# A transformer block on one core: small work moved behind the row maxima, GpSimd in a written order, and the last phase's weights loaded and split one step apart

## The chip, the core and the metric

The kernel runs on one core of a Trainium2 chip. A core has five engines with their own instruction queues: TensorE (PE in the profile, its weight loads PEld), VectorE (DVE), ScalarE (ACT), GpSimd (POOL) and SyncE (SP), which only issues DMA transfers. Each queue runs in order, and an instruction that has to wait holds everything behind it on its engine. Engines meet through semaphores. The metric is the device time of one execution in microseconds, a median of several runs.

## The reference

The output is `x + attention(xn) + glu(xn)`, with `xn` the layer norm of `x` (2048 rows of 640, float32):

```python
xn = _layernorm(x)                                   # rows of 640
q, k, v = split(xn @ wqkv)                           # 32 heads of 20
scores = einsum("bhqd,bhkd->bhqk", q, k) * 20 ** -0.5
scores = where((i - j >= 0) & (i - j < 256), scores, -1e9)
attention = einsum("bhqk,bhkd->bhqd", softmax(scores), v) @ wo
glu = (gelu(xn @ w_gate) * (xn @ w_up)) @ w_down     # 1728 wide
out = x + attention + glu
```

## The kernel before

Every float32 product is made of three matmuls: both operands are split in a high part (a ScalarE copy to `F32R`) and a low part (the remainder, a subtraction on VectorE or GpSimd), and high·high, low·high and high·low are added up in PSUM.

The kernel has four stretches in time. The first (to about 88 us) makes the layer norm and the first projections. The second, `attention()` (about 88 to 660 us), works through 32 units `u`: eight groups of four heads times four chunks of 512 rows. Each unit has `NS = 14` slots, and `now[0]` counts slots. TensorE's order in a slot is written out: on even slots two score pieces for the exponentials (`exp_piece`, PSUM tag `ex`, two buffers) and two or three pieces for the row maxima of a unit further on (`max_piece`, tag `mx`, three buffers); in every slot about three steps of a filler (`pull_fill`): the projections of q, k and v and the gate and up products of the GLU. At slot 0 of the next unit comes `av_unit`, probabilities times `v`.

Small work hangs on a table `acts`, from slot to functions: `defer(n, fn)` puts `fn` n slots later, and `tick()` hands out what is due at the start of a slot, ahead of the slot's score and maximum pieces. There:

- `max_piece` (L428) computes scores into PSUM; VectorE's `tensor_tensor_reduce` (L444) adds the mask and takes the row maximum. A PSUM buffer is free again when VectorE has read it.
- `max_end` (L453) turns the negated maxima with one matmul (L456), ScalarE copies them to `mr` (L458), and SyncE sends them into two rows of the unit's `qs` (L459), where the score matmuls add them.
- `save_qk` (L215) drains a projection: ScalarE's copy `upper` (L236), VectorE's remainder (L237), ScalarE's second copy (L224), GpSimd's last remainder (L225), then stores to `qd` or `kd` (L231).
- `gate_up_fill` (L550) makes GELU by hand in steps `c1` to `c5`, alternating ScalarE and VectorE, and stores to `hd` (L581).
- `load_stack` (L414) reads `qd` and `kd` back for unit `u + 3` (six DMAs, L422).
- `exp_piece` (L483) takes the exponential on ScalarE (L496) and clears with GpSimd's `affine_select` (L502, L505) what lies outside the window, in three banks of probabilities.
- `av_unit` (L509) copies its result on ScalarE (L520) and stores it by five DMAs (L522, L523).
- `load_v` (L245) loads and splits the second half of the v weights; `x_sums` (L619) makes sums of `xn` on GpSimd (L643) and stores them (L646).

`tc.manual_schedule(engines=MANUAL)` keeps TensorE, ScalarE and VectorE in the written order there; GpSimd's and SyncE's instructions are placed by the framework's scheduler.

The third stretch (660 to 843 us) makes the rest of gate and up in pairs of chunks. The fourth, the last phase (from 843 us), is the product with `w_down` and `wo`: 80 steps `n`, ten for each of eight blocks `p` of 256 rows, one of the ten an `"e"` step with eight matmuls. A "plain" step (all of `p = 0`, the first four of `p = 1`) has 24 matmuls of 320 columns; every other has 21, with sums of operands in seven products, Strassen's way. Step `n` loads the operand of step `n + 4` (L1029, buffers `hr`), splits that of `n + 2` (`split_step`, three buffers `at`), splits a weight quad of 128 x 1280 if one is due (`high_quad` on ScalarE, L930, in step `n`; `low_quad` on VectorE, by `sub`, L937, in step `n + 1`) and fetches another quad (`fetch`, L915, three buffers `stg`). The quads `b4` to `b8` are first used in steps 5 to 9, the quads `t4` to `t8` from step 15 on, `t0` to `t3` from step 26 on. After a block's last step `drain` adds the PSUM banks to the output rows on VectorE, and TensorE must wait for a bank to be added up before the next block writes to it.

Of the kernel before, what the change touches and what calls it, by code (L numbers as in the profile page):

```python
# [24 lines left out]
NF = 14  # L25
# [36 lines left out]
def block_kernel(ctx, tc, x, wqk, wv, wgu, wdo, wdl, out):  # L62
# [131 lines left out]

    def defer(n, fn, *a):
        if now[0] is None:
            fn(*a)
        else:
            at(now[0] + n, fn, *a)
# [17 lines left out]
    def save_qk(t, c, ps):  # L217
# [5 lines left out]
        def lower():  # L223
            nc.scalar.activation(pt[:, 1, :], r, AF.Copy)  # L224
            nc.gpsimd.tensor_tensor(out=pt[:, l, :], in0=r, in1=pt[:, 1, :], op=OP.subtract)  # L225
            a, end = t % 5 * 128, t % 5 * 128 + 128
# [7 lines left out]

        def upper():
            nc.scalar.activation(pt[:, h, :], ps, AF.Copy)  # L236
            nc.vector.tensor_tensor(out=r, in0=ps, in1=pt[:, h, :], op=OP.subtract)  # L237
            defer(1, lower)
# [3 lines left out]
    def load_v(h, res, rpool=None):  # L242
# [185 lines left out]
    def max_piece(u, i):  # L428
# [5 lines left out]
        ps = psm.tile([128, 384], F32, name="ps_m", tag="mx")  # L434
# [11 lines left out]
        if i == 15:  # L446
            mx = maxes.pop(u)
            nm = nms[u % 2]
            nc.vector.tensor_scalar(nm[:, 0, 0], mx, -1.0, None, op0=OP.mult)
            nc.vector.scalar_tensor_tensor(nm[:, 0, 1], mx, -1.0, nm[:, 0, 0], op0=OP.mult, op1=OP.subtract)  # L450
            maxes[u] = nm

    def max_end(u):  # L453
# [5 lines left out]
        nc.sync.dma_start(qs[u % NQ][120:122].rearrange("p j t -> p (j t)"), mr)  # L459
# [20 lines left out]
    def exp_piece(u, s):  # L480
# [16 lines left out]
        if j == 3:  # L497
            for p in bank:
                for col, diag in diag_tail(*p, c):
                    a = pt[:, :, col:col + 128]  # L500
                    if diag:
                        nc.gpsimd.affine_select(out=a, in_=a, pattern=[[0, 4], [1, 128]], compare_op=OP.is_ge,  # L502
                                                fill=0.0, base=0, channel_multiplier=-1)
                    else:
                        nc.gpsimd.affine_select(out=a, in_=a, pattern=[[0, 4], [-1, 128]], compare_op=OP.is_ge,  # L505
                                                fill=0.0, base=-1, channel_multiplier=1)

    def av_unit(u):
# [12 lines left out]
        for j in range(4):  # L521
            nc.sync.dma_start(od[c].rearrange("(d h) t -> h d t", h=H)[4 * g + j], ob[32 * j:32 * j + DH, :])  # L522
        nc.sync.dma_start(sd[c][4 * g:4 * g + 4, :], ob[DH::32, :])  # L523
# [27 lines left out]
    def gate_up_fill(f, ws, c):  # L551
# [4 lines left out]
        def c1():  # L556
# [4 lines left out]
            defer(1, c2)  # L561
# [809 lines left out]
```

## Time and profile before

| | |
|---|---|
| three runs | 1089.28, 1089.98 and 1090.28 us; median 1089.98 us |
| the profiled execution | 1090.18 us, its span 1088.4 us |
| granted TensorE clock | 0.999 |
| TensorE busy | 1070.2 us, 98% of the span, 7253 matmuls |
| VectorE, ScalarE, GpSimd busy | 762.3, 511.8 and 334.6 us |
| all DMA | 162.31 MB, 149 GB/s on average |

Matmuls are pipelined, and the profile models their ends, so two neighbours overlap on paper and a busy TensorE is not one at its peak. "Idle before" an instruction is the time in which its engine had nothing in work, with what ended it. SyncE's rows are its sequencer's: an issue, and not the transfer.

### The profile page before, as it was taken

Reading aid. Unit: us, or ns where it says so; the run is one execution under the profiler, and the core shown is the slowest. Engines: PE = TensorE matmul, PEld = TensorE weight load, DVE = VectorE, ACT = ScalarE, POOL = GpSimd, SP = SyncE. Lnnn points to the kernel's source line nnn. Section 1 sums busy time; section 2 is a strip of 40 time slices with the busy share of each in tenths; the row PEclk is TensorE's granted clock in tenths of the full one; section 3 lists DMA queues with packets and bytes.
Section 4 is the critical chain, followed back from the end, with each engine's and each line's share of the span. In section 5 each row is a group of like instructions: output and inputs, shape, how many; then the busy total and the mean of one; then the engine's idle time right before and its main releaser. Section 6 shows DMA issues by size and latency. Waiting matters only on the chain.

```text
span 1088.4 us, 20870 instructions
## 1 busy us (share of the span) xinstructions
PE 1070.2 (98%) x7253; PEld 856.8 (79%) x7253; DVE 762.3 (70%) x2030; ACT 511.8 (47%) x1037; POOL 334.6 (31%) x513
## 2 busy tenths in 40 slices
PE   8999999999999999999999999999999999999998
PEld 7887667666678766666666677888888999999998
DVE  7756667566666575666666636788775779888887
ACT  4434655465645456555555465332223554333332
POOL 5045634566726444655344241121110000000000
PEclk9999999999999999999999999999999999999999
DMA  5642343446442333353332316488775884343443
GB/s 202 200 137 82 114 142 92 129 130 181 142 132 65 94 109 117 117 163 104 111 112 84 98 51 203 150 279 292 242 256 177 281 289 163 92 137 121 134 125 115
DMA packets 96058, 162.31 MB, mean 149 GB/s; under 512 B 13248, under 2 KB 57920, under 8 KB 95952
## 3 DMA queue, kind: packets, MB, share of 16 engines
q1 hardware_dynamic: 95952, 160.97, 46.8%
q8 instruction: 57, 0.93, 0.4%
q14 instruction: 49, 0.40, 0.1%
HBM read 104.40 MB, written 56.23 MB: 148 GB/s over the span
## 4 chain that ended last, share of the span: by engine, by line
PE 80%; DVE 9%; DMA 4%; ACT 3%; issue 2%; SPq 1%; POOL 1%; DVEq 0%; ACTq 0%
PE ps_d L101 23%; PE ps L1100 16%; PE ps_g L844 14%; PE ps_o L516 7%; PE ps_e L494 7%; PE ps_m L442 7%; PE ps_v L101 5%; PE ps_g L101 1%; DVE junk L444 1%; DVE ss L937 1%; DMA hr<-od 1%; ACT P L496 1%; DMA od<-ato 1%; DVE at L937 1%; ACT at L1054 1%
## 5 line engine op out<-in xcount | busy, mean ns | idle before, releaser
L444 DVE CUSTOM_DVE_ANT_0 junk<-ps_m,mask 128x384 bf16<-128x384 f32 (+2 forms) x512 | 271.8, 531 | 177.4 <-PE ps_m L442 136.2
L496 ACT ACTIVATE P<-ps_e 128x512 f32<-128x512 f32 (+2 forms) x384 | 197.6, 568 | 63.6 <-PE ps_e L494 57.4
L1100 PE MATMUL ps<-wb,at 128*128 128x320 f32 x999 | 156.9, 310 | 3.3 <-DVE xr L1120 2.8
L1100 PEld LDWEIGHTS ps<-wb,at 128*128 128x128 f32 x999 | 148.9, 188 | 4.5 <-DVE xr L1120 3.3
L502 POOL TENSOR_SCALAR_AFFINE_SELECT P<-P 128x512 f32<-128x512 f32 x128 | 83.7, 654 | 176.4 <-ACT P L496 169.2
L101 PE MATMUL ps_d<-xh,wql 128*128 128x512 f32 x430 | 129.3, 410 | 0.0
L101 PE MATMUL ps_d<-xl,wqh 128*128 128x512 f32 x430 | 128.6, 408 | 0.0
L101 PE MATMUL ps_d<-xh,wqh 128*128 128x512 f32 x430 | 128.5, 409 | 0.0
L442 PE MATMUL ps_m<-ks,qs 120*128 120x128 bf16 (+1 forms) x704 | 120.9, 275 | 3.6 <-DVE mx L444 1.8
L494 PE MATMUL ps_e<-qs,ks 122*128 122x128 bf16 (+2 forms) x704 | 113.1, 277 | 1.5 <-ACT P L496 0.8
L494 PEld LDWEIGHTS <-ks 122*128 122x128 bf16 x704 | 50.2, 98 | 55.2 <-issue 44.5
L101 PEld LDWEIGHTS ps_d<-xh,wql 128*128 128x128 f32 x430 | 77.9, 189 | 15.8 <-issue 2.3
L101 PEld LDWEIGHTS ps_d<-xl,wqh 128*128 128x128 f32 x430 | 78.3, 188 | 14.8 <-issue 0.6
L1100 PE MATMUL ps<-wt,at 128*128 128x320 f32 x552 | 89.1, 309 | 0.0
L101 PEld LDWEIGHTS ps_d<-xh,wqh 128*128 128x128 f32 x430 | 77.7, 189 | 14.1 <-ACT xh L185 0.3
L442 PEld LDWEIGHTS <-qs 120*128 120x128 bf16 x704 | 62.1, 98 | 32.7 <-issue 13.8
L516 PE MATMUL ps_o<-P,v 128*32 128x384 f32 (+2 forms) x1408 | 84.3, 386 | 0.0
L505 POOL TENSOR_SCALAR_AFFINE_SELECT P<-P 128x512 f32<-128x512 f32 x112 | 72.3, 656 | 37.3 <-ACT P L496 37.3
L1100 PEld LDWEIGHTS ps<-wt,at 128*128 128x128 f32 x552 | 82.9, 188 | 0.3 <-DVE u L937 0.3
L1054 ACT ACTIVATE at<-ss 128x512 fp32r<-128x512 f32 x59 | 37.3, 632 | 90.1 <-DVE ss L937 89.8
L516 PEld LDWEIGHTS ps_o<-P,v 128*32 128x32 f32 x1408 | 40.1, 110 | 39.5 <-issue 29.2
L225 POOL TENSOR_TENSOR pt<-r,pt 128x512 bf16<-128x512 f32 x40 | 46.7, 1168 | 79.2 <-ACT pt L224 79.1
(185 smaller groups left out, 1692.8 us busy)
## 6 DMA issues: line engine op xcount, KB each, us to landing
hr<-hd SPq DMA_DIRECT2D x104, 128.0 KB
hd<-he SPq DMA_DIRECT2D x50, 256.0 KB
wr<-wgu SPq DMA_DIRECT2D x27, 320.0 KB
qs<-qd SPq DMA_DIRECT2D x32, 240.0 KB
ks<-kd SPq DMA_DIRECT2D x32, 240.0 KB
ats<-wdo SPq DMA_DIRECT2D x9, 640.0 KB
wtd<-ats SPq DMA_DIRECT2D x9, 640.0 KB
stg<-wtd SPq DMA_DIRECT2D x9, 640.0 KB
```

The source lines that it names most:

```text
L101: nc.tensor.matmul(ps, a(k), b(k), start=n == 0, stop=n == 3 * nk - 1)
L225: nc.gpsimd.tensor_tensor(out=pt[:, l, :], in0=r, in1=pt[:, 1, :], op=OP.subtract)
L442: nc.tensor.matmul(ps[:, lo:hi], lh, rhs, start=True, stop=True)
L444: nc.vector.tensor_tensor_reduce(out=junk[:, 0:n], in0=ps[:, 0:n], in1=mask[:, 384 - n:384], scale=1.0, scalar=NEG, op0=OP.add, op1=OP.max ...
L494: nc.tensor.matmul(ps[:, col:col + n], k[0:QROWS, j, kc:kc + 128], q[0:QROWS, j, q0:q0 + n], start=True, stop=True)
L496: nc.scalar.activation(pt[:, j, lo:hi], ps[:, lo:hi], AF.Exp, scale=SCALE)
L502: nc.gpsimd.affine_select(out=a, in_=a, pattern=[[0, 4], [1, 128]], compare_op=OP.is_ge, fill=0.0, base=0, channel_multiplier=-1)
L505: nc.gpsimd.affine_select(out=a, in_=a, pattern=[[0, 4], [-1, 128]], compare_op=OP.is_ge, fill=0.0, base=-1, channel_multiplier=1)
L516: nc.tensor.matmul(o[32 * j:32 * j + 32, q0:q0 + n], v[:, w0_:w0_ + 32], pt[:, j, col:col + n], start=i == 0, stop=i == len(todo) - 1, ski ...
L844: nc.tensor.matmul(ps, i, j, start=first and n == 0, stop=n == len(work) - 1, skip_group_check=True)
L1054: nc.scalar.activation(hi[:, 3:7], s, AF.Copy)
L1100: nc.tensor.matmul(ps[bank][:, 0:HD], *work[bank][j], start=bank not in begun, stop=final[p, bank] == n and j == len(work[bank]) - 1, skip ...
```

## The change

In the attention stretch:

- A list `lates`: what is handed to `late()` runs at `flush()`, after the slot's score and maximum pieces and ahead of the filler. VectorE's remainder of `save_qk`, its steps `c2`, `c4` and `c5` of the GELU, and the negation of the maxima go there, and so does the DMA of `mr`, which ScalarE issues now.
- Two of the sixteen maximum pieces of a unit (in slots 6 and 10) use the PSUM buffer of `av_unit`'s output instead of one of the three.
- Stores come later: those of `save_qk` and `hd` by one slot, `x_sums` by two, `av_unit` by three. `load_stack` is called in slot 12 instead of 11, the clearing of the probabilities one slot after the exponentials; the last step of `save_qk` one slot later, too. `max_end` comes last of what is due in a slot.
- GpSimd's order is the written one.
- The second half of the v weights is split in the third set of the filler instead of the fourth, with its loads issued a step later in the code, and set `("qk", 4)` changes places with `("gu", 1)`.

In the last phase, quads are split in steps 1 to 13 and 15 instead of 1, 3 to 6, 8, 10 to 15, 20 and 22; each is fetched two steps ahead, and ScalarE issues the fetches from step 2 on. The first addition of `drain` (bank 2) moves into `split_step`, between VectorE's sums and its remainders. TensorE's order of matmuls is the same in both programs.

```diff
+    lates = []
+    def late(fn, *a):
+        if now[0] is None or now[0] < NS:
+            fn(*a)
+        else:
+            lates.append((fn, a))
...
         def lower():
             nc.scalar.activation(pt[:, 1, :], r, AF.Copy)
             nc.gpsimd.tensor_tensor(out=pt[:, l, :], in0=r, in1=pt[:, 1, :], op=OP.subtract)
+            defer(1, store)
...
+        def middle():
+            nc.vector.tensor_tensor(out=r, in0=ps, in1=pt[:, h, :], op=OP.subtract)
+            defer(1 if now[0] is None or now[0] < NS else 2, lower)
+
         def upper():
             nc.scalar.activation(pt[:, h, :], ps, AF.Copy)
-            nc.vector.tensor_tensor(out=r, in0=ps, in1=pt[:, h, :], op=OP.subtract)
-            defer(1, lower)
+            late(middle)
...
         for k in range(KT):
+            if rpool is None and 0 < k < KT - 1:
+                raws.append(get(k + 1))
...
-            if k + 2 < KT:
+            if rpool is not None and k + 2 < KT:
                 raws.append(get(k + 2))
...
-        ps = psm.tile([128, 384], F32, name="ps_m", tag="mx")
+        pool, tag = where
+        ps = pool.tile([128, 384], F32, name="ps_m", tag=tag)
...
-        nc.sync.dma_start(qs[u % NQ][120:122].rearrange("p j t -> p (j t)"), mr)
+        late(lambda: nc.scalar.dma_start(qs[u % NQ][120:122].rearrange("p j t -> p (j t)"), mr))
...
         if j == 3:
-            for p in bank:
...
+            defer(1, clear, u, bi)
...
-        for j in range(4):
-            nc.sync.dma_start(od[c].rearrange("(d h) t -> h d t", h=H)[4 * g + j], ob[32 * j:32 * j + DH, :])
...
+        defer(3, store)
...
-            defer(1, c2)
+            defer(1, late, c2)
...
-            defer(1, c3)
+            defer(2, c3)
...
-            defer(1, c4)
+            defer(1, late, c4)
...
-    sets = [("qk", 1), ("gu", 0), ("qk", 2), ("qk", 3), ("gu", 1), ("qk", 4)]
-    sets += [("gu", f) for f in range(2, NFA)] + [("gu", NF - 1)]
+    sets = [("qk", 1), ("gu", 0), ("qk", 2), ("qk", 3), ("qk", 4)]
+    sets += [("gu", f) for f in range(1, NFA)] + [("gu", NF - 1)]
...
     def tick():
-        return [y for t in sorted(t for t in acts if t <= now[0]) for y in acts.pop(t)]
+        todo = [y for t in sorted(t for t in acts if t <= now[0]) for y in acts.pop(t)]
+        return sorted(todo, key=lambda y: y[0] is max_end)
...
-                    pull_max(3 if i in (6, 12) else 2, T)
-                if i == 11 and 3 <= u + 3 < NU:
+                    pull_max(3 if i in (6, 12) else 2, T, {6: 1, 10: 0}.get(i))
+                flush()
+                if i == 12 and 3 <= u + 3 < NU:
                     load_stack(u + 3)
                 pull_fill(RATE / NS)
...
-    with tc.manual_schedule(engines=MANUAL):
+    with tc.manual_schedule(engines=MANUAL | {mybir.EngineType.Pool}):
         attention()
...
         sub(s[:, 3], raw[:, 3], s[:, 2], OP.add)
+        if behind:
+            behind()
         nc.scalar.activation(hi[:, 3:7], s, AF.Copy)
...
+    def first_add(ps, xt):
+        sub(xt[:, 1, 0:HD], ps[2][:, 0:HD], xt[:, 1, 0:HD], OP.add)
...
-        add(1, 1, b[2])
         if p == NP - 1:
+            add(1, 1, b[2])
             add(1, 1, a)
...
+    order_ = [("b", q) for q in range(4, NQD)] + [("t", q) for q in (4, 5, 6, 7, 8, 0, 1, 2)]
+    tasks = {n + 1: q for n, q in enumerate(order_)}
+    tasks[len(order_) + 2] = "t", 3
+    turns = list(tasks)
+    fetch_at = {0: [tasks[n] for n in turns[1:3]]}
+    for i, n in enumerate(turns[3:]):
+        fetch_at.setdefault(turns[i] + 1, []).append(tasks[n])
...
-        if n in fetch_at:
-            fetch(*fetch_at[n])
+        for q in fetch_at.get(n, ()):
+            fetch(*q, eng=nc.scalar if n else nc.sync)
...
-            split_step(n + 2, (lambda: first_copy(p, ps)) if turn_ else None)
+            split_step(n + 2, *((lambda: first_copy(p, ps), lambda: first_add(ps, xr)) if turn_ else ()))
```

More of the change, by code (lines that the diff above doesn't have):

```diff
@@ L426, in block_kernel, with max_piece @@
     maxes = {}
-    def max_piece(u, i):
+    def max_piece(u, i, where):
         g, c = divmod(u, NC)
@@ L497, in exp_piece, with clear @@
         if j == 3:
-            for p in bank:
[L499 to L506, printed above, removed]
+            defer(1, clear, u, bi)
+    def clear(u, bi):
+        c = u % NC
+        pt = pts[u, bi]
+        for p in pieces(c)[bi]:
+            for col, diag in diag_tail(*p, c):
+                a = pt[:, :, col:col + 128]
+                if diag:
+                    nc.gpsimd.affine_select(out=a, in_=a, pattern=[[0, 4], [1, 128]], compare_op=OP.is_ge,
+                                            fill=0.0, base=0, channel_multiplier=-1)
+                else:
+                    nc.gpsimd.affine_select(out=a, in_=a, pattern=[[0, 4], [-1, 128]], compare_op=OP.is_ge,
+                                            fill=0.0, base=-1, channel_multiplier=1)
     def av_unit(u):
@@ L687, in block_kernel, with pull_max @@
     debt = [0.0]
-    def pull_max(n, slot):
-        for _ in range(n):
+    def pull_max(n, slot, other=None):
+        for k in range(n):
             x = next(stream, None)
@@ L901, in four, with fetch @@
         return t.rearrange("p k (h n) -> p (k h) n", h=2)
-    def fetch(kind, q, where="stg"):
+    def fetch(kind, q, where="stg", eng=nc.sync):
         if where == "wr":
@@ L914, in fetch @@
         t = pool.tile([128, 4, HD], F32, name="stg", tag=where, bufs=bufs)
-        nc.sync.dma_start(t, four(wdo[q]) if kind == "b" else wtd[q])
+        eng.dma_start(t, four(wdo[q]) if kind == "b" else wtd[q])
         if kind == "t" and q in borrow:
@@ L1029, in load_step, with split_step @@
             nc.sync.dma_start(flat[:, 256 * i:256 * i + 256], src[:, t0:t0 + 256])
-    def split_step(n, between=None):
+    def split_step(n, between=None, behind=None):
         p, k = steps[n]
```

39 lines of the change are left out of this document (23 added, 16 removed).

## The prediction

> **What bounds the kernel now.** I read the page's first part, then TensorE's waits, then the busy time by stretch.
>
> ```profile
> PE 1070.2 (98%) x7253; PEld 856.8 (79%) x7253; DVE 762.3 (70%) x2030; ACT 511.8 (47%) x1037; POOL 334.6 (31%) x513
> ...
> PE ps L1100 <- DVE xr L1120: 2.8, 2, 1.5
> PE ps_m L442 <- DVE mx L444: 1.8, 5, 0.7
> PE ps_m L442 <- DMA od<-ob: 1.3, 1, 1.3
> PE ps_e L494 <- ACT P L496: 0.8, 2, 0.4
> PE ps L1100 <- DVE at L937: 0.5, 2, 0.3
> PE ps_v L101 <- DVE v L290: 0.2, 1, 0.2
> ...
> 88.00:660.00 572.00, 566.73 (x4304) 398.31 (x4303) 360.15 (x1187) 314.17 (x650) 287.77 (x455) 1.00 0.38 114
> 843.00:876.00 33.00, 33.00 (x226) 32.93 (x224) 22.89 (x28) 16.52 (x22) 0.00 (x0) 1.00 0.86 285
> 876.00:941.00 65.00, 61.72 (x414) 60.47 (x413) 55.69 (x117) 30.66 (x55) 0.00 (x0) 1.00 0.55 179
> ```
>
> The first row is busy time of each engine; the next six are what TensorE waited for (us in all, times, longest); the last three are stretches: length, then busy time of PE, PEld, DVE, ACT and POOL, clock, DMA share, GB/s. TensorE is the bound: it idles 18 us in all, and the change leaves its instructions and their order alone. So at most the idle time in the two stretches that it touches can be won, and a loss can only be a new wait. In attention TensorE idles 572.00 - 566.73 = 5.3 us: 4.1 in nine listed waits (1.8 + 1.3 + 0.8 + 0.2), the rest in gaps that the waits do not list. In the last phase it idles 65.00 - 61.72 = 3.3 us between 876 and 941, which is the two rows of L1100 (2.8 + 0.5).
>
> A wait costs more than its idle column, since modelled ends reach into it:
>
> ```profile
> 906.36 1.04 PE L1100 MATMUL ps<-wb,at 128*128 128x320 f32 x6
> 908.92 0.71 PE L1100 MATMUL ps<-wb,at 128*128 128x320 f32 x3 [1.52 <-DVE xr L1120]
> ...
> 940.52 144.54 PE ps L1100 x982
> ```
>
> The chain of waits has 982 matmuls in 144.54 us, 0.147 us each. Six of them from 906.36 end at 907.24; the next begins at 908.92, 1.68 later, against 1.52 in brackets. I add 0.16 us a wait.
>
> **Attention, part by part.** *VectorE's waits.* What they look like:
>
> ```profile
> 120.00 0.69 DVE L237 TENSOR_TENSOR r<-ps_d,pt 128x512 f32<-128x512 f32 x1 [0.90 <-ACT pt L236]
> 120.61 0.55 DVE L444 CUSTOM_DVE_ANT_0 junk<-ps_m,mask 128x384 bf16<-128x384 f32 x1
> ...
> 121.67 0.56 DVE L444 CUSTOM_DVE_ANT_0 junk<-ps_m,mask 128x384 bf16<-128x384 f32 x1 [0.51 <-PE ps_m L442]
> ...
> 122.29 0.32 PE L442 MATMUL ps_m<-ks,qs 120*128 120x384 bf16 x1 [0.67 <-DVE mx L444]
> ```
>
> VectorE waited 0.90 us for ScalarE's copy, then spent 0.6 us on the remainder, and only then took a maximum that was ready; the three buffers ran out, and TensorE stood. Afterwards the remainder, `c2`, `c4` and `c5` go behind the slot's maxima, and two pieces of sixteen have a fourth buffer. The five waits cost 1.8 + 5 x 0.16 = 2.6 us. Between none and all of it can go; I take 2.4, since the order of VectorE is exactly what made them. What covers the delay of the remainder: its PSUM buffer is needed again five slots later (15 filler steps at 3 a slot; a slot is 572 / 32 / 14 = 1.3 us), and it comes less than one slot later.
>
> *The wait of 1.3 us.* The profile names an `od` store, but the instruction reads `qs` and `ks`:
>
> ```profile
> 459.63 0.68 SPq L459 DMA_DIRECT2D qs<-mr  x1
> 463.89 0.78 SPq L231 DMA_DIRECT2D kd<-pt  x2
> 464.76 1.38 SPq L422 DMA_DIRECT2D qs<-qd  x3
> ...
> 472.27 0.33 PE L442 MATMUL ps_m<-ks,qs 120*128 120x128 bf16 x2 [1.34 <-DMA od<-ob]
> ```
>
> SyncE held the loads (L422) behind a `kd` store whose data GpSimd was late with (nothing is issued from 460.3 to 463.89). With stores called later than their producers SyncE seldom stands before the loads, though they are called a slot later. All of 1.3 + 0.16 = 1.5 us goes; the other bound is that the slot is lost, 1.3 us more.
>
> *Other items.* The 0.8 us behind the exponentials stays: ScalarE's work ahead of them is the same. The 0.2 us behind `v` stays. Of the 5.3 - 4.1 = 1.2 us in unlisted gaps I take 0.5; the bounds are 0 and 1.2. The DMA of `mr` costs ScalarE about the 0.68 us of its SyncE row, 32 times, in slot 10, where ScalarE has no exponentials for three slots (it is busy 314 of 572 us). Its data has time:
>
> ```profile
> 600.29 0.27 ACT L458 ACTIVATE mr<-ps_n 32x128 bf16<-32x128 f32 x1 [1.17 <-PE ps_n L456]
> 600.47 0.62 ACT L496 ACTIVATE P<-ps_e 128x256 f32<-128x256 f32 x2
> 601.98 0.68 SPq L459 DMA_DIRECT2D qs<-mr  x1
> ...
> 606.84 0.61 PE L494 MATMUL ps_e<-qs,ks 122*128 122x128 bf16 x4
> ```
>
> ScalarE would issue at about 601.1, sooner than SyncE's 601.98, and the first matmul that reads it comes at 606.84. If ScalarE is held there (the program lets a DMA wait for the one eight before it, usually on SyncE's queue), cover is 4 us. GpSimd in hand order and the clearing one slot later: from slot 11 to `av_unit`'s third bank are three slots and most of the product, about 5.5 us, for two selects of 0.65 us:
>
> ```profile
> L502 POOL TENSOR_SCALAR_AFFINE_SELECT P<-P 128x512 f32<-128x512 f32 x128 | 83.7, 654 | 176.4 <-ACT P L496 169.2
> ```
>
> Nothing, unless GpSimd's queue is 4 us behind; both ends are priced as a rival. The v weights and the order of sets move work between slots with cover on both sides: nothing. Attention: -2.4 - 1.5 - 0.5 = -4.4 us.
>
> **The last phase.** Its waits cost 3.3 + 4 x 0.16 = 3.9 us now. All come from VectorE:
>
> ```profile
> 907.78 0.69 DVE L937 TENSOR_TENSOR at<-ss,at 128x512 fp32r<-128x512 f32 x1 [0.23 <-ACT at L1054]
> 908.39 0.88 DVE L1120 TENSOR_TENSOR xr<-ps,xr 128x320 f32<-128x320 f32 x2
> ...
> 930.08 0.43 DVE L937 TENSOR_TENSOR ss<-hr 128x256 f32<-128x256 f32 x1
> 932.58 0.42 DVE L937 TENSOR_TENSOR ss<-hr 128x256 f32<-128x256 f32 x1
> 940.52 0.71 PE L1100 MATMUL ps<-wb,at 128*128 128x320 f32 x3 [1.24 <-DVE xr L1120]
> ```
>
> A step with sums takes VectorE 932.58 - 930.08 = 2.50 us, TensorE 21 x 0.147 = 3.09; a `drain` from 908.39 takes 5.6. Over a block (nine such steps, an "e" step) VectorE has 28.5 us of work for 29.0, so each weight remainder (1.4 us net) after step 13 becomes lag. Now six fall there: four in steps 13 to 16, two in 21 and 23. Afterwards three, in 13, 14 and 16. By step 22 VectorE is one remainder, 1.4 us, ahead of now, and in block 2 two remainders, 3.0 us: the second wait for a split (0.5 - 0.3 = 0.2) and the one at 940.52 (0.2 + 1.24 + 2 x 0.16 = 1.8 us) go. `first_add`, ahead of 1.2 us of remainders, gives bank 2 back sooner.
>
> Against that stands step 10. Now:
>
> ```profile
> 853.11 1.49 DVE L937 TENSOR_TENSOR wb<-stg,wb 128x1280 fp32r<-128x1280 f32 x1
> ...
> 860.11 0.33 SPq L915 DMA_DIRECT2D stg<-wdo  x1
> 865.49 1.27 ACT L930 ACTIVATE wb<-stg 128x1280 fp32r<-128x1280 f32 x1 [1.58 <-DMA stg<-wdo]
> 872.77 0.63 ACT L1044 ACTIVATE at<-hr 128x512 fp32r<-128x512 f32 x1 [0.90 <-PE ps L1100]
> 874.04 1.48 DVE L937 TENSOR_TENSOR wt<-stg,wt 128x1280 fp32r<-128x1280 f32 x1
> 875.45 1.68 DVE L1120 TENSOR_TENSOR xr<-ps,xr 128x320 f32<-128x320 f32 x4
> 876.29 0.63 ACT L1044 ACTIVATE at<-hr 128x512 fp32r<-128x512 f32 x1 [2.89 <-PE ps L1100]
> ```
>
> TensorE ends step 9 at 876.3, and bank 2 is added up at 875.9: 0.3 us to spare. Afterwards ScalarE's fetch in step `n` waits until VectorE's `low_quad(n - 1)` has read the buffer. The fetch of step 2 waits for the remainder at 853.11 and goes out at 854.6 to 855.0. From there a step is a loop: ScalarE's copy 0.6, VectorE's remainder 0.6, `low_quad` 1.4, issue 0.33 and handoffs of 0.1 to 0.2: 3.2 us, against 24 x 0.147 = 3.5 of TensorE. Step 3 begins on ScalarE at 855.0, step 9 so at 874.3, not 872.77, and the first addition at 877.0: TensorE waits 0.7 to 1.3 us at step 10, nothing if the issue is free, some 1.6 if loads are slower. I take 1.0, near the upper rows, since each of the loop's parts has a row. Then VectorE also starts the steps with sums up to 2 us later than now, which uses up its 1.4 us: steps 20 to 22 cost 1.6 instead of 1.52 + 0.3 + 2 x 0.16 = 2.1. So 2.6 us of waits in place of 3.9: -1.3, between -3.9 (no loop) and +2 (a late loop and full lag).
>
> The DMA share of 0.86 in the row from 843 to 876 counts against it. The Trainium skill says (DMA: Bandwidth & Descriptors, "Issuing engines are not separate DMA queues") that transfers from any engine run on the same 16 DMA engines, and issuing from two saves only the issue time. By that rule nothing lands sooner for being issued by ScalarE, which is the second rival.
>
> **The sum.** From the profiled execution's 1090.18: -4.4 - 1.3 = -5.7, 1084.5; that execution is 0.2 above the median, so 1084.3. From no measurable change this kernel's runs tell about 0.2%, 2.2 us. If every wait of both stretches and the unlisted gaps went: 5.3 + 9 x 0.16 + 3.9 = 10.6, 1079.5.
>
> **The rivals.** *GpSimd in a row (slower).* An instruction whose input is late holds the clearing behind it, and `av_unit` waits in most of the 32 units. It decides once the queue is more than 4 us behind in slot 11; 0.35 us a unit are 11 us: 1084.3 + 11 = 1095. For it: GpSimd is busy 41.37 of 58 us in its fullest stretch,
>
> ```profile
> 241.00:299.00 58.00, 57.24 (x418) 39.23 (x416) 36.68 (x123) 35.80 (x73) 41.37 (x60) 1.00 0.53 158
> ```
>
> against it, it mostly idles for ScalarE's exponentials (176.4 us ahead of L502), and no wait of TensorE names it now.
>
> *The last phase runs at the loads' pace.* Eleven loads of 640 KB come in steps 2 to 12 instead of up to step 20. At 285 GB/s for 0.86, all engines carry 331; a step wants 0.66 + 0.26 MB, 0.92 / 331 = 2.8 us of 3.5, and rows of `x` and `out` fill the rest. A load took 860.11 to 865.5, 5.4 us; two are under way, so a step needs (5.4 + 1.3 + 0.3) / 2 = 3.5. At 6.5 us, 4.1: over nine steps 5 us of new waits; 1089.3, no change. Above 8 us it would be slower. That its small operand loads no longer queue behind the quads speaks against it.
>
> *The waits only move.* VectorE's postponed work holds the next slot's maxima, and only SyncE's 1.5 and the last phase's 1.3 remain: 1087.2.
>
> **How the numbers follow.** Forecast 0.58 (all faster); waits move 0.14 (two thirds faster); loads' pace 0.12 (mostly the same); GpSimd 0.16 (slower). Faster 0.58 + 0.09 + 0.02 = 0.69; same 0.05 + 0.09 = 0.14; slower 0.16 + 0.01 = 0.17. The forecast's own range is 1079.5 to 1087.5; the range from 1079.5 to 1091.5 takes in the two middle rivals and leaves out most of GpSimd's 0.16 and little below.
>
> **What would show it.** TensorE's waits for `mx` near 0 and none on `qs` or `ks` loads; none of `ps_o` on `P`; ScalarE's `mr` DMA ahead of the next exponentials; a wait of about 1 us at step 10 (near 876), one below 1.5 at step 20, none at the end of block 2. Waits of `ps_o` in every unit, or operand splits that come late in each of steps 5 to 12, would prove me wrong.

## The result, and the profile after

| | median us (runs) | ratio to before, 95% interval |
|---|---|---|
| before, same session | 1089.86 (20) | |
| changed | 1087.72 (20) | 0.9981 [0.9974, 0.9988] |
| forecast | 1084.3 | 0.995 |

The change gained 2.1 us where 5.7 were forecast. The profiled execution of the changed kernel spans 1086.3 us (1088.4 before). First TensorE's waits in the changed kernel (us in all, times, longest), by the line numbers after (L464/L466 the maxima's matmul and its reduction, L970 `high_quad`, L955 `fetch`, L977 `sub`, L1084 and L1088 the first copy of a plain split and of one with sums, L1142 the last phase's matmul, L1165 an addition of `drain`):

```profile
PE ps L1142 <- ACT wb L970: 2.2, 1, 2.2
...
PE ps_m L464 <- DVE mx L466: 1.1, 3, 0.5
PE ps L1142 <- ACT at L1088: 0.8, 1, 0.8
PE ps L1142 <- DVE xr L977: 0.8, 1, 0.8
PE ps L1142 <- DVE xr L1165: 0.8, 1, 0.8
PE ps L1142 <- DVE at L977: 0.7, 3, 0.3
...
PE ps_n L482 <- DVE nm L475: 0.5, 2, 0.3
PE ps_v L101 <- DVE v L311: 0.3, 1, 0.3
PE ps L1142 <- ACT m L1153: 0.2, 1, 0.2
```

Attention shows 1.9 us of waits where 4.1 stood, and no row for the `qs` and `ks` loads or the exponentials. The last phase shows 5.5 us in eight waits where 3.3 in four stood; with the prediction's 0.16 a wait, 6.8 for 3.9. So the two stages went opposite ways. The timelines say where. Before (start, duration, [idle before <- what ended it]):

```profile
790.04 0.73 PE L844 MATMUL ps_g<-xh,s4h 128*128 128x512 f32 x2 [0.82 <-DVE qp L847]
...
843.24 2.06 PE L1100 MATMUL ps<-wb,at 128*128 128x320 f32 x13
```

After:

```profile
837.79 2.50 PE L1142 MATMUL ps<-wb,at 128*128 128x320 f32 x16
...
850.09 0.63 ACT L1084 ACTIVATE at<-hr 128x512 fp32r<-128x512 f32 x1 [0.78 <-ACT w L1337]
...
856.22 0.34 ACTq L955 DMA_DIRECT2D stg<-wtd  x1
...
861.97 1.28 ACT L970 ACTIVATE wt<-stg 128x1280 fp32r<-128x1280 f32 x1 [1.40 <-DMA stg<-wtd]
...
870.97 1.48 DVE L977 TENSOR_TENSOR wt<-stg,wt 128x1280 fp32r<-128x1280 f32 x1
872.37 1.68 DVE L1165 TENSOR_TENSOR xr<-ps,xr 128x320 f32<-128x320 f32 x4
872.88 1.89 SPq L1168 DMA_DIRECT2D out<-xr  x4
872.96 0.63 ACT L1084 ACTIVATE at<-hr 128x512 fp32r<-128x512 f32 x1
873.00 14.31 PE L1142 MATMUL ps<-wb,at 128*128 128x320 f32 x96 [2.20 <-ACT wb L970]
...
874.75 1.28 ACT L970 ACTIVATE wt<-stg 128x1280 fp32r<-128x1280 f32 x1 [1.16 <-DMA stg<-wtd]
880.25 0.34 ACTq L955 DMA_DIRECT2D stg<-wtd  x1
880.71 0.63 ACT L1084 ACTIVATE at<-hr 128x512 fp32r<-128x512 f32 x1 [4.69 <-DMA out<-xr]
...
892.38 0.41 PE L1142 MATMUL ps<-wb,at 128*128 128x320 f32 x1 [0.81 <-ACT at L1088]
...
907.91 0.71 PE L1142 MATMUL ps<-wb,at 128*128 128x320 f32 x3 [0.80 <-DVE xr L977]
909.38 2.22 PE L1142 MATMUL ps<-wt,at 128*128 128x320 f32 x12 [0.76 <-DVE xr L1165]
```

The last phase is reached 843.24 - 837.79 = 5.45 us sooner; 0.98 of that is the wait on `qp` at 790, which has gone; the rest is attention. (The wait on `qp` cannot be credited to the change: `e16_last_sync_all`, below, whose attention and third stretch are those of the kernel before, has none there either.) Then two things happen in the last phase. ScalarE's splits of operands run in the loop that the prediction describes, 850.09 to 872.96 in seven steps, 3.27 us each. (In some of these steps the last thing ahead of the split is not the fetch but the copy of the quad, which itself waited for its load: 1.40 us at 861.97. Those loads went out at the loop's pace, so this trace alone does not part the two.) VectorE's first addition of `drain` begins at 872.37, behind the `low_quad` from 870.97: TensorE waits 2.20 + 0.16 = 2.36 us at step 10. (The profile names `wb`; what comes last is more likely the bank: the first addition ends at 872.86, TensorE starts 0.14 us later, and in `e6_last_sync`, where the profile names the addition, the distance is the same.) And from 876.03, the end of the copy from 874.75, ScalarE does nothing until 880.25, when it issues the fetch of `t1`: the splits behind it, and VectorE's work behind these, stay late to the end of the second block (892 to 910).

Idle columns hide stalls that modelled ends cover, so below I also use *excess*: for each pair of neighbouring matmuls the time from start to start, less the lower quartile of such pairs in the kernel before, where it is over 0.02 us. In the last phase (from 845 us) it sums to 4.80 us before and 8.14 after: 3.3 lost. All 7253 matmuls have the same shapes and tiles in the same order in every run, so a stage can also be timed from one matmul to the same one. From the matmul that starts at 88.1 us in the kernel before to the one at 660.1, attention takes 572.0 us before and 567.5 after: 4.5 gained. With the 0.9 of the third stretch, 4.5 + 0.9 - 3.3 = 2.1 is the difference of the two profiled executions.

### The profile page after: what moved, and what is told of

The parts are those of the page before. It is cut to its first block, busy times and chain, and to the rows that moved or that the text cites. A ratio compares the mean times of both kernels' runs of the same rounds, so it can differ in the third digit from the quotient of the medians.

```text
span 1086.3 us, 20868 instructions
## 1 busy us (share of the span) xinstructions
PE 1068.9 (98%) x7253; PEld 856.2 (79%) x7253; DVE 766.0 (71%) x2030; ACT 511.9 (47%) x1037; POOL 340.7 (31%) x513
## 4 chain that ended last, share of the span: by engine, by line
PE 84%; DVE 8%; DMA 4%; issue 1%; ACT 1%; SPq 0%; POOL 0%; ACTq 0%; DVEq 0%
PE ps_d L101 25%; PE ps L1142 15%; PE ps_g L884 15%; PE ps_o L547 8%; PE ps_e L520 7%; PE ps_m L464 7%; PE ps_v L101 5%; DVE junk L466 2%; PE ps_g L101 1%; DMA stg<-wtd 1%; DMA stg<-wdo 1%; DMA xi<-x 1%; PE ps_t L177 1%; DMA out<-xr 1%; DVE xi L160 1%
## 5 line engine op out<-in xcount | busy, mean ns | idle before, releaser
L466 DVE CUSTOM_DVE_ANT_0 junk<-ps_m,mask 128x384 bf16<-128x384 f32 (+2 forms) x512 | 271.9, 531 | 177.8 <-PE ps_m L464 132.9
L1142 PE MATMUL ps<-wb,at 128*128 128x320 f32 x999 | 157.8, 310 | 4.8 <-ACT wb L970 2.2
L1142 PEld LDWEIGHTS ps<-wb,at 128*128 128x128 f32 x999 | 149.0, 188 | 6.9 <-ACT wb L970 2.4
L533 POOL TENSOR_SCALAR_AFFINE_SELECT P<-P 128x512 f32<-128x512 f32 x128 | 86.6, 676 | 159.1 <-ACT P L522 155.0
L464 PE MATMUL ps_m<-ks,qs 120*128 120x128 bf16 (+1 forms) x704 | 120.1, 275 | 1.4 <-DVE mx L466 1.1
L1142 PE MATMUL ps<-wt,at 128*128 128x320 f32 x552 | 89.0, 309 | 0.8 <-DVE xr L1165 0.8
L464 PEld LDWEIGHTS <-qs 120*128 120x128 bf16 x704 | 62.2, 98 | 29.2 <-issue 11.6
L1142 PEld LDWEIGHTS ps<-wt,at 128*128 128x128 f32 x552 | 82.9, 188 | 1.2 <-DVE xr L1165 1.0
L536 POOL TENSOR_SCALAR_AFFINE_SELECT P<-P 128x512 f32<-128x512 f32 x112 | 73.7, 668 | 27.9 <-ACT P L522 27.8
```

The costliest lines, as they stand in the source:

```text
L464: nc.tensor.matmul(ps[:, lo:hi], lh, rhs, start=True, stop=True)
L466: nc.vector.tensor_tensor_reduce(out=junk[:, 0:n], in0=ps[:, 0:n], in1=mask[:, 384 - n:384], scale=1.0, scalar=NEG, op0=OP.add, op1=OP.max ...
L1142: nc.tensor.matmul(ps[bank][:, 0:HD], *work[bank][j], start=bank not in begun, stop=final[p, bank] == n and j == len(work[bank]) - 1, skip ...
```

## The experiments

*Stage by stage, and who issues the fetches.* `e1_attention` is the change up to attention with the old last phase, `e2_last` the reverse. `e3_sync` and `e4_behind` edit the changed kernel:

```diff
e3_sync
-            fetch(*q, eng=nc.scalar if n else nc.sync)
+            fetch(*q)
e4_behind
-        for q in fetch_at.get(n, ()):
-            fetch(*q, eng=nc.scalar if n else nc.sync)
...
             split_step(n + 2, *((lambda: first_copy(p, ps), lambda: first_add(ps, xr)) if turn_ else ()))
+        for q in fetch_at.get(n - 1, ()):
+            fetch(*q, eng=nc.scalar if n > 1 else nc.sync)
         prepare(n)
```

> The change up to the end of the attention stage alone; the last phase is that of the kernel before. Theory A (the two stages add up: attention gained some 4.5 us and the wait of 1.0 on qp near 790 us went with it, the last phase lost some 3.3): 4.5 to 5.5 us faster than before, so some 3 us faster than the whole change. Rival (the last phase costs more only because it is reached sooner, with loads less far ahead): about 2 us faster, as the whole change, with TensorE's waits in the last phase grown from 3.9 to over 6.

> The change of the last phase alone. Theory A: 2 to 3.5 us slower than before, with a wait of 2 to 2.5 us at step 10 and late splits in steps 15 to 17. The prediction's own account: 1.3 us faster. The rival of e1: no change within 1 us.

> The changed kernel, with all fetches of the last phase issued by SyncE. Theory A (ScalarE's order makes a loop of 3.3 us a step, and a fetch waiting at step 10 holds it for 4 us): the wait at step 10 falls from 2.4 to below 1, the splits of steps 15 to 17 are in time, and the kernel is 2 to 4 us faster than the changed one, unless SyncE, held in ScalarE's place, brings the small operand loads late. Rival B (the loads' pace): the wait at step 10 stays at 2 us or more and the time stays within 1 us.

> The changed kernel, with ScalarE's fetch moved behind the next step's first split copy, so that VectorE's weight remainder before it is done when its turn comes. Theory A: the loop is broken, the split copies of steps 5 to 12 run at TensorE's pace or ahead of it, the wait at step 10 falls from 2.4 to below 0.7, and the kernel is 1.5 to 2.5 us faster than the changed one. Rival B (the loads' pace): loads that go out up to a step later bring the weight copies later, and the wait at step 10 stays or grows.

| | median us | ratio to before | excess in the last phase |
|---|---|---|---|
| e1_attention | 1085.58 | 0.9963 [0.9948, 0.9978] | 4.05 |
| e2_last | 1092.67 | 1.0031 [1.0019, 1.0043] | 8.38 |
| e3_sync | 1082.62 | 0.9933 [0.9919, 0.9948] | 1.57 |
| e4_behind | 1089.50 | 0.9992 [0.9979, 1.0006] | 7.60 |

The stages add up: attention alone wins 4.0 us, a little less than expected, and the last phase alone loses 3.4. (The 8.38 of `e2_last` holds some 1.5 us of matmuls at half the granted clock, 878.6 to 882.0; see the last section.) `e3_sync` decides between theory A and the loads' pace: with the same schedule, only issued by SyncE, the last phase loses 1.57 us in all, and the kernel is 7.3 us faster than before. Its timeline:

```profile
860.87 1.28 ACT L970 ACTIVATE wt<-stg 128x1280 fp32r<-128x1280 f32 x1 [1.09 <-DMA stg<-wtd]
861.97 0.32 SPq L955 DMA_DIRECT2D stg<-wtd  x1
...
863.87 1.27 ACT L970 ACTIVATE wt<-stg 128x1280 fp32r<-128x1280 f32 x1 [1.21 <-DMA stg<-wtd]
864.77 21.04 PE L1142 MATMUL ps<-wb,at 128*128 128x320 f32 x142
...
866.76 1.28 ACT L970 ACTIVATE wt<-stg 128x1280 fp32r<-128x1280 f32 x1 [1.09 <-DMA stg<-wtd]
...
903.70 2.22 PE L1142 MATMUL ps<-wt,at 128*128 128x320 f32 x12 [0.43 <-DVE xr L1165]
```

A quad lands every 2.9 to 3.0 us (copies at 860.87, 863.87, 866.76), and TensorE passes step 10 without a wait: 142 matmuls in a row. So the loads' pace is not the bound; that rival falls. A load takes 4.5 to 4.8 us to its copy when SyncE issues it from 859 us on (861.97 to 866.76 is 4.8), and 5.2 to 5.8 from ScalarE (856.22 to 861.97 is 5.75). By the Trainium skill (DMA: Bandwidth & Descriptors, "Issuing engines are not separate DMA queues") a second issuing engine saves only its issue time. The runs agree in that nothing lands sooner for it (5.75 us against 4.8).

`e4_behind` was to break the loop and did not:

```profile
857.85 1.27 ACT L970 ACTIVATE wb<-stg 128x1280 fp32r<-128x1280 f32 x1 [3.46 <-DMA stg<-wdo]
...
883.01 0.33 ACTq L955 DMA_DIRECT2D stg<-wtd  x1
883.38 1.27 ACT L970 ACTIVATE wt<-stg 128x1280 fp32r<-128x1280 f32 x1 [3.70 <-DMA out<-xr]
```

The edit also sent the first loads a step later, and ScalarE waited for their landing (3.46 us) with the next split behind it. So it does not separate the theories. But the hold is there again, now until 883.01.

*The loop and the hold apart.* In the built program each DMA of SyncE and ScalarE waits, before it is issued, for the one eight places earlier in the two queues together, whose semaphore it takes over. For the fetch of `t1` in the changed kernel that is the second of the four stores of `out` issued from 872.88 on: the trace shows the same semaphore for both, its last update by the store comes at 880.15, and the fetch goes out at 880.25. Two runs put half of the fetches back:

```diff
e5_first_sync
-            fetch(*q, eng=nc.scalar if n else nc.sync)
+            fetch(*q, eng=nc.scalar if n > 9 else nc.sync)
e6_last_sync
-            fetch(*q, eng=nc.scalar if n else nc.sync)
+            fetch(*q, eng=nc.scalar if 0 < n < 10 else nc.sync)
```

> The changed kernel, with the fetches of steps 2 to 9 issued by SyncE and those from step 10 on by ScalarE. Theory A1 (ScalarE's loop of 3.27 us a step makes the wait at step 10): that wait falls from 2.4 to below 0.5. Theory A2 (the hold of 4.2 us comes from the fetch of t1, which waits for the semaphore that it shares with the second of the four stores of out issued just before): here the fetch of t1 shares its semaphore with a small load that landed long before, so ScalarE is not held for more than 2 us, and the time is that with all fetches on SyncE, within 1.5 us (about 7 below the kernel before). If the hold comes from elsewhere (an instruction fetch, the stores themselves), it is there again, and the time is about 4 below the kernel before.

> The other half: the fetches of steps 2 to 9 on ScalarE as in the changed kernel, those from step 10 on by SyncE. Theory A1: the wait at step 10 stays at 2.2 to 2.5 us. Theory A2: ScalarE is not held after it, the splits of steps 15 to 17 come in time, the waits between 892 and 910 (3.8 us in all) fall below 1.5; the kernel is 4 to 5 us faster than the kernel before. If ScalarE's late start alone makes all of these waits, they stay, and the time is that of the changed kernel.

`e5_first_sync`: 1083.77 us, 0.9944 [0.9929, 0.9959], excess 3.16. Its timeline:

```profile
867.82 17.52 PE L1142 MATMUL ps<-wb,at 128*128 128x320 f32 x118
...
874.37 0.34 ACTq L955 DMA_DIRECT2D stg<-wtd  x1
...
890.31 0.53 ACT L1088 ACTIVATE at<-hr 128x384 fp32r<-128x384 f32 x1 [3.55 <-DMA hr<-od]
...
903.36 0.71 PE L1142 MATMUL ps<-wb,at 128*128 128x320 f32 x3 [0.80 <-DVE xr L977]
```

`e6_last_sync`: 1085.21 us, 0.9951 [0.9937, 0.9965], excess 4.10. Its timeline:

```profile
875.37 0.33 ACTq L955 DMA_DIRECT2D stg<-wtd  x1
875.80 0.63 ACT L1084 ACTIVATE at<-hr 128x512 fp32r<-128x512 f32 x1 [1.16 <-issue]
875.84 8.37 PE L1142 MATMUL ps<-wb,at 128*128 128x320 f32 x45 [1.82 <-DVE xr L1165]
```

In the first the wait at step 10 is gone, and ScalarE, still the issuer from step 10 on, is not held (`t1` goes out at 874.37, since its semaphore there belongs to a small load that had landed). What stays is 1.9 us at step 20, two waits that the changed kernel has too (907.91 and 909.38); ahead of them ScalarE waited 3.55 us for a small load, but that this makes them is not isolated. In the second the wait at step 10 stays (1.82 + 0.16). Behind it TensorE ran at half the granted clock for 3.4 us, which nothing in the program asks for:

```profile
876.00:880.00 4.00, 4.00 (x18) 4.00 (x18) 3.09 (x8) 1.59 (x2) 0.00 (x0) 0.57 0.81 206
```

(length, busy time and count of PE, PEld, DVE, ACT and POOL, clock, DMA share, GB/s). That is some 1.5 of the 4.10; otherwise 0.5 us is left behind step 10 of what was 8.14 - 2.36 = 5.8. So the wait at step 10, which goes with ScalarE's fetches up to step 9, is 2.4 us of excess in the changed kernel; the hold is 8.14 - 2.36 - 3.16 = 2.6; and 3.16 - 1.57 = 1.6 more stay while ScalarE issues from step 10 on. By the ratios, against 2.1 us for the whole change, `e6_last_sync` is 5.3 us faster than before, `e5_first_sync` 6.1 and `e3_sync` 7.3. Theories A1 and A2 both stand, with that rest open.

*The new schedule itself.* `e16_last_sync_all` is the kernel before with the new last phase, fetches on SyncE; `e7_no_first_add` is `e3_sync` with the first addition back in `drain`:

```diff
e7_no_first_add
-            split_step(n + 2, *((lambda: first_copy(p, ps), lambda: first_add(ps, xr)) if turn_ else ()))
+            split_step(n + 2, *((lambda: first_copy(p, ps), None) if turn_ else ()))
...
+        add(1, 1, b[2])
         if p == NP - 1:
-            add(1, 1, b[2])
```

> The kernel before with the new schedule of the last phase alone, all fetches on SyncE. From the stalls of the last phase with SyncE's fetches (1.1 to 1.6 us) against those before (4.8): 3 to 3.7 us faster than before. Rival (it needs attention's shorter stage ahead of it): 1 to 2 us.

> All fetches on SyncE, and the first addition of a block's end back in its old place, behind the next step's remainders. Theory: at the end of the second block VectorE gives bank 2 back 1.2 us later, so the wait there (0.4 to 0.6) becomes 1.2 to 1.6; 0.5 to 1.2 us slower than with all fetches on SyncE alone. Rival: with one weight quad split a step VectorE is ahead anyway, and it makes no difference.

`e16_last_sync_all`: 1088.40 us, 0.9978 [0.9965, 0.9990], 2.4 us faster, between the two expectations; its excess is 2.06, 2.7 below before. `e7_no_first_add`: 1083.51 us, 0.9940 [0.9926, 0.9954]; the wait at the end of the second block grows from 0.59 to 0.91 us, so the first addition is worth 0.3 us there, and the time cannot tell it. So what gains is the even spread of the weight quads, with the fetches that go with it.

*Attention, part by part*, all but `e15_fourth` on `e3_sync`. `e8_no_late` lets `late` call at once; `e11_three` takes the fourth buffer away; `e12_no_late_three` does both; `e15_fourth` gives the kernel before the fourth buffer and nothing else; `e14_lower_soon` is `e8_no_late` with ScalarE's waiting copies one slot after VectorE's work again:

```diff
e8_no_late
-        if now[0] is None or now[0] < NS:
-            fn(*a)
-        else:
-            lates.append((fn, a))
+        fn(*a)
e11_three
-                    pull_max(3 if i in (6, 12) else 2, T, {6: 1, 10: 0}.get(i))
+                    pull_max(3 if i in (6, 12) else 2, T)
e14_lower_soon
-            defer(1 if now[0] is None or now[0] < NS else 2, lower)
+            defer(1, lower)
-            defer(2, c3)
+            defer(1, c3)
```

> All fetches on SyncE, and in attention the remainders and the other work that was put behind a slot's maxima ahead of them again; all other parts stay. The prediction's account: TensorE's waits for the maxima (1.1 us in three with them behind) grow to 2 to 3 us, 1 to 2.4 us slower than with all fetches on SyncE alone. Rival: the fourth buffer for two of sixteen pieces, which stays, is what shortened these waits, and they stay at 1.1.

> All fetches on SyncE, and in attention no fourth buffer: all sixteen pieces of maxima in the three old ones; the postponed work stays behind the maxima. The run without postponing had left TensorE's stalls in attention as they were (10.0 us against 11.3). Theory C (the fourth buffer shortened the waits): the waits for maxima grow from 1.1 to 2 to 3 us, and the kernel is 1 to 2 us slower than with all fetches on SyncE alone. Prediction's account (the order on VectorE did it): they stay at 1.1.

> All fetches on SyncE, and neither postponing nor the fourth buffer. If the two together made the gain at the maxima, TensorE's waits for them go back to 1.8 us in five or more, and its stalls in attention rise by 2 to 2.5 us over the 10.0 to 11.3 of the runs that have one of the two. If it is neither (the stores, or GpSimd's order), they stay below 1.3.

> The kernel before with the fourth buffer for two of sixteen pieces of maxima, and nothing else. Theory C: TensorE's waits for maxima fall from 1.8 us in five to below 0.7, its stalls in attention by 1.5 to 2.5 us, and the time by 1 to 2.5. Prediction's account (the order on VectorE made the waits): they stay above 1.2.

> All fetches on SyncE, no postponing, and ScalarE's copies that need a remainder of VectorE one slot after it again instead of two. Theory E (such a copy, waiting for VectorE, held the exponentials behind it; in the kernel before two such copies had waited 1.9 us just ahead of the two waits): TensorE's waits for P of ScalarE come back, 0.4 to 1 us. Rival (the later place of the maxima's last copy in a slot freed them): none.

Excess over 0.1 us in attention, by what TensorE was about to do (us, times); "maxima" counts `max_piece` and the turning matmul of `max_end`, and `mr` is a matmul that waits for the DMA of `mr`. The column "attention" is that stage from matmul to matmul, as above:

| | maxima | exponentials | loads | mr | attention, us | median us, ratio |
|---|---|---|---|---|---|---|
| before | 4.4 (15) | 3.3 (11) | 1.5 | 0 | 572.0 | 1089.86 |
| changed | 3.9 (13) | 0.7 (3) | 0 | 0 | 567.5 | 1087.72 |
| e3_sync | 4.0 (13) | 0.7 (3) | 0 | 0.4 | 567.9 | 1082.62, 0.9933 |
| e8_no_late | 4.0 (10) | 0 | 0 | 0 | 566.6 | 1082.24, 0.9918 [0.9906, 0.9931] |
| e11_three | 6.6 (19) | 0.7 (3) | 0 | 0 | 570.1 | 1085.81, 0.9961 [0.9946, 0.9976] |
| e12_no_late_three | 6.4 (19) | 0 | 0 | 0 | 569.2 | 1082.99, 0.9937 [0.9924, 0.9949] |
| e15_fourth | 2.7 (6) | 3.2 (11) | 1.8 | 0 | 570.4 | 1088.35, 0.9980 [0.9971, 0.9990] |
| e14_lower_soon | 2.3 (8) | 4.0 (11) | 0 | 0.6 | 569.4 | 1083.25, 0.9932 [0.9915, 0.9949] |

TensorE's waits, first the row for the maxima in `e12_no_late_three`:

```profile
PE ps_m L461 <- DVE mx L463: 3.1, 10, 0.4
```

the same row in `e8_no_late`:

```profile
PE ps_m L461 <- DVE mx L463: 2.3, 4, 1.2
```

and the row for the exponentials in `e14_lower_soon`:

```profile
PE ps_e L517 <- ACT P L519: 1.8, 3, 1.0
```

With the fourth buffer the row for the maxima falls from ten waits to four; the row for the exponentials is 0.8 in two before and absent from the changed kernel. Three readings. Putting VectorE's work behind the maxima changed that column by 0.0 to 0.2 us (4.0 against 4.0, 6.4 against 6.6) and left 0.7 us at the exponentials: it gained nothing. The 0.0 hides two parts. `max_piece` alone waits less with postponing (3.0 us against 4.0, without the fourth buffer 5.8 against 6.4), but the negation of the maxima is postponed too, and the turning matmul waits 0.9 us for it in three places, where it waits for nothing in the other rows of the table. The fourth buffer is worth 1.7 to 2.6 us, with postponing or without, and in the kernel before as well (by the whole stage 2.2, 2.6 and 1.6). And moving ScalarE's copies to two slots after VectorE's remainder freed the exponentials (4.0 to 0), at the price of 1.7 at the maxima. The kernel before shows such a copy just ahead of one of its two listed waits:

```profile
244.04 0.63 ACT L224 ACTIVATE pt<-r 128x512 bf16<-128x512 f32 x1 [1.95 <-DVE r L237]
244.57 0.64 ACT L496 ACTIVATE P<-ps_e 128x256 f32<-128x256 f32 x2
```

*The loads' wait and GpSimd.* `e9_stores_now` (on `e3_sync`) calls all stores right after their producers, `e10_pool_auto` (on `e3_sync`) leaves GpSimd's order in attention to the planner; `e13_stores_pool` does both on `e8_no_late`, with the clearing back in its old slot. `e17_old_sets` and `e18_load_slot` undo one part each on `e8_no_late`:

```diff
e9_stores_now
-            defer(1, store)
+            store()
-        defer(3, store)
+        store()
-            defer(1, lambda: nc.sync.dma_start(hd[f][c], st["t"]))
+            nc.sync.dma_start(hd[f][c], st["t"])
-            defer(2, lambda: nc.sync.dma_start(td[p][i][:, k, half * w:half * w + w], t))
+            nc.sync.dma_start(td[p][i][:, k, half * w:half * w + w], t)
e10_pool_auto
-    with tc.manual_schedule(engines=MANUAL | {mybir.EngineType.Pool}):
+    with tc.manual_schedule(engines=MANUAL):
e13_stores_pool: both, and
-            defer(1, clear, u, bi)
+            clear(u, bi)
e17_old_sets
-    sets = [("qk", 1), ("gu", 0), ("qk", 2), ("qk", 3), ("qk", 4)]
-    sets += [("gu", f) for f in range(1, NFA)] + [("gu", NF - 1)]
+    sets = [("qk", 1), ("gu", 0), ("qk", 2), ("qk", 3), ("gu", 1), ("qk", 4)]
+    sets += [("gu", f) for f in range(2, NFA)] + [("gu", NF - 1)]
-                    if i == 2 or i == 3 and c == 0:
+                    if i == 3:
-                    if i == 3 and c == 0:
+                    if i == 3 and c < 2:
e18_load_slot
-                if i == 12 and 3 <= u + 3 < NU:
+                if i == 11 and 3 <= u + 3 < NU:
```

> All fetches on SyncE, and the stores of attention's filler work (kd, od, sd, hd, td) called right after their producers again. Prediction's account: SyncE stands behind a store again, a wait of about 1.3 us on the qs and ks loads comes back, 1 to 1.5 us slower than with all fetches on SyncE alone. Rival: GpSimd, in hand order, brings the kd data sooner, and nothing comes back.

> All fetches on SyncE, and GpSimd's order in attention left to the program's planner again. Prediction's account: no difference within 0.5 us. Rival (the hand order brings the kd data and the cleared P sooner): a wait on the qs and ks loads comes back, or ps_o on P, 0.5 to 2 us slower than with all fetches on SyncE alone.

> All fetches on SyncE, no postponing behind the maxima, and both the deferred stores and GpSimd's hand order with the later clearing undone. Theory D (these two do the same job: SyncE stands behind a kd store when GpSimd brings its data late, so either GpSimd's order or the later call cures it): the wait of about 1.3 us on the qs and ks loads comes back. Rival (another part, such as the loads' new slot, cured it): none comes back.

> All fetches on SyncE, no postponing, and the filler's sets in their old order (the second gate and up set ahead of the last q and k set), with the weight preparations where they were. Theory F (the new order has the last q and k set's kd data ready long before the loads): the wait of about 1.3 us on the qs and ks loads comes back. Rival (the loads' later slot keeps SyncE from standing ahead of them): none comes back.

> All fetches on SyncE, no postponing, and the loads of the next stack called in slot 11 again instead of 12. Theory F: no wait on the loads. Rival: one of about 1.3 us.

Medians and ratios: `e9_stores_now` 1084.13, 0.9939 [0.9927, 0.9951]; `e10_pool_auto` 1088.19, 0.9981 [0.9970, 0.9992]; `e13_stores_pool` 1094.94, 1.0035 [1.0023, 1.0047]; `e17_old_sets` 1084.28, 0.9945 [0.9931, 0.9959]; `e18_load_slot` 1082.68, 0.9930 [0.9918, 0.9943].

The wait on the `qs` and `ks` loads came back in none of the five. So it stays away without any one of these parts, and without those of `e13_stores_pool` together; what cured it is open. `e9_stores_now` is 1.5 us slower than `e3_sync`, as the prediction's account had it, but not by that wait: 0.6 us more of its profiled attention (568.5) is a wait for `mr`. GpSimd's order showed something else. TensorE's waits in `e10_pool_auto` in attention:

```profile
PE ps_o L547 <- POOL P L533: 2.9, 1, 2.9
```

and in `e13_stores_pool`:

```profile
PE ps_o L544 <- POOL P L533: 3.7, 3, 2.0
PE ps_o L544 <- POOL P L530: 2.9, 1, 2.9
```

In the changed attention, GpSimd in the planner's order clears `P` too late, 2.9 us once or 6.6 us in four places; in hand order never, and in the kernel before, in the planner's order, never either. Which other part of the change brings this out is not isolated. Attention takes 571.4 us in `e10_pool_auto`, 3.6 more than in `e3_sync`, and 579.9 in `e13_stores_pool`, where two stretches of 3.4 us at half clock add to the waits.

## Why the prediction was right and wrong

The direction was right, in part by luck: of the 2.1 us between the profiled executions 0.9 is the wait on `qp`, which is not the change's. The size was wrong in one step, the last phase: forecast -1.3 us, measured +3.3 (excess 4.80 to 8.14). In its terms:

- *Step 10, "I take 1.0": 2.36.* The mechanism was right and so was the pace, 3.27 us a step for 3.2. The loop began later: the split copy at 850.09 is 1.8 us behind TensorE's step 3, not 1.2, and 0.07 us in each of seven steps adds 0.5; the remaining 0.3 is not accounted for.
- *The hold at step 10: no term at all.* The prediction knew that the program lets a DMA wait for the one eight before it, and used it for the `mr` DMA in attention, but did not ask it of the fetches, which stand right behind four stores. That is 2.6 us of excess, the largest single piece. With 1.6 more that stays while ScalarE issues from step 10 on, it turned "steps 20 to 22 cost 1.6" into waits from 892 to 916.
- *VectorE's relief* (one quad split a step) was real: without ScalarE's fetches the last phase's waits fall by 2.7 to 3.2 us (`e16_last_sync_all`, `e3_sync`), between the 3.9 - 1.6 = 2.3 that the sum counts beside step 10 and the 3.9 of its "no loop" end. No wait stands at the end of block `p = 2`, as said.

Attention came out as forecast, 4.5 us for 4.4, but by other terms:

- *VectorE's waits, -2.4:* in excess 4.4 to 3.9. The step "the order of VectorE is exactly what made them" fell: the order is worth 0.6 to 1.0 us at `max_piece`, which the postponed negation and the exponentials take back. The fourth buffer, which the prediction mentions beside it, is the part that works, and other parts of the change take most of it back (6.6 without it, 4.4 before).
- *The loads, -1.5:* right in size; the reason given, the deferred stores, is not shown: with the stores called at once the wait did not come back.
- *"The 0.8 us behind the exponentials stays":* wrong; 3.3 to 0.7. ScalarE's work ahead of them is the same, but two slots behind VectorE's remainder it no longer waits there for VectorE; one slot behind, in `e14_lower_soon`, they wait 4.0 us.
- *`mr` on ScalarE at nothing:* from 0 to 1.5 us in the runs with attention as in the changed kernel (0 in it, 0.4 in `e3_sync`, 1.5 in `e1_attention`), where before there was none.
- *GpSimd, v weights and sets at nothing:* true together. The slower rival, GpSimd in a row, did not come; the waits of `ps_o` on `P` that it named came where the hand order was taken away.
- *The wait on `qp` at 790* (0.98) went too, which no step foresaw. It comes and goes: 0.3 us is listed again in `e5_first_sync` and `e7_no_first_add`, 0.7 in `e10_pool_auto`, and none in `e16_last_sync_all`, with the third stretch of before.

The rival "the waits only move" gave 1087.2, close to 1087.72, by luck: postponed work did not hold the next maxima (`max_piece` waits less with it), though what it gained there moved to the turning matmul and the exponentials; attention gained 4.5 us instead of 1.5, and the last phase lost 3.3 instead of gaining 1.3. "The loads' pace" fell with `e3_sync`.

The lowest median is that of `e8_no_late`, the changed kernel with the fetches on SyncE and without postponing: 1082.24 us, 0.8% below before. The times do not tell it from `e3_sync` (1082.62).

## What to carry to other kernels

Before a DMA is moved to a compute engine's queue, find out what it waits for when issued, the completion of an earlier DMA whose semaphore it reuses included: on SyncE such a wait delays loads that are steps ahead, on ScalarE it stops the splits that TensorE needs next. If a schedule and an issuer are changed together, price them apart: here, in the stalls of the profiled executions, the schedule gained 2.7 to 3.2 us and the issuer lost 6.6 (5.2 by the ratios). A buffer more was worth some 2 us where a reordering of the engine that empties the buffers was worth nothing.

## What was not expected of the hardware

Small stores took long. The four stores of `out` (512 packets of 1280 bytes), issued from 872.88 on, moved their first packet at 876.3 in the changed kernel's trace, 95% of them by 878.9 and the last at 880.6; it is this tail that held ScalarE. The last sixteenth of the packets came up to 2 us behind the rest. In `e3_sync` the same stores were issued from 871.43 on and moved from 874.8 to 878.3. Both began 3.4 us after the issue; over all twenty traces it was 2.95 to 3.42.

In some executions TensorE runs at half the granted clock for 3.4 or 6.8 us, beginning between 10.7 and 13.8 us, and the program gets some 13 matmuls less far in the first 88 us (518 against 531 in the two runs below). The stretch in `e3_sync` (length, then busy time and count of PE, PEld, DVE, ACT and POOL; then clock, DMA share, GB/s):

```profile
13.00:20.00 7.00, 6.26 (x53) 6.09 (x53) 5.49 (x16) 2.78 (x8) 7.00 (x8) 1.00 0.34 108
```

and in `e10_pool_auto`:

```profile
13.00:20.00 7.00, 6.26 (x30) 6.08 (x30) 5.94 (x15) 2.63 (x7) 7.00 (x8) 0.51 0.43 127
```

It costs as much as the effects studied here: the first stretch ends 2.6 us later in the second (91.3 against 88.7 us for the same matmul). So of the 7.3 us between these two profiled executions 2.6 are the clock and 3.6 attention, and the 5.6 between the medians need not be GpSimd's order alone. The same happens elsewhere: in `e2_last` and `e6_last_sync` the half clock starts 0.6 us behind the wait at step 10 (2.5 and 1.8 us idle), while the changed kernel and `e4_behind`, with 2.2 and 3.2 us idle there, keep the full clock. What lowers it is open.
